# Splitting a weight load by rows, meant for the DMA engines that end first, a shorter last load, and one output store in place of two

## The chip, the cores and the metric

The kernel runs on one core of one Trainium2 chip. The metric is the device time of one execution in microseconds (us), the median of several runs. A profiled execution also has a *span*, from the first to the last instruction that the profile counts; the span is about 2.1 us shorter than the device time. A run is called fast when it lies within 1.5% of the fastest of the same kernel.

## The reference, cut to what matters

```python
# A: 32 heads, 32768 keys each; B: 32 query heads, 8 key/value heads, the last 4096 keys
q = (x @ wq) ...                        # one token
p = softmax(q @ k_cache^T * Dh ** -0.5)
o = p @ v_cache
return o.reshape(1, 1, 4096) @ wo       # wo: 4096 x 512, once for A and once for B
# out = concat([a, b], axis=-1)         # 1 x 1 x 1024, bf16
```

Nearly all of the time goes into reading the caches of A, 537 MB. The change touches only what comes after: the 4 MB of `A_wo` and the 512 outputs of A.

## The kernel before

All large loads are issued by SyncE (SP) into one DMA queue, one behind the other (q1 of the page: 570.43 of 570.59 MB). `A_wo` lies in SBUF as 128 partitions ("rows") of 32 chunks, 512 bf16 values (1 KB) per chunk and row. It is loaded in five parts, cut along the chunks, so that TensorE (PE) can start on a part when that part has landed.

```python
    def load(self, dst, src, sem, *deps):
        self.op("sp", lambda e: e.dma_start(dst, src).then_inc(sem, 16), *deps)

    WO_CUTS = {"A": (0, 11, 19, 25, 29, 32), "B": (0, 16, 32)}

    def load_wo(self, name, part):
        a0, a1 = self.WO_CUTS[name][part:part + 2]
        src = self.X[name]["wo"].rearrange("(p a) c -> p (a c)", a=32)
        ...
        self.load(self.kbuf[:, off + 512 * a0:off + 512 * a1], src[:, 512 * a0:512 * a1], self.wosem[name][part],
                  self.free["k"][t])
```

The projection works off the parts in turn. Part 0 of A goes as full-width matmuls into a bank of its own (line 745 of the kernel before, 746 after). The later chunks go as two half-width matmuls side by side, into partitions 0 and 64 of one bank (`halves`, line 719 before, 724 after). Ahead of part 3 the result of part 0 is added in by an fp32 matmul. Each half is then cast into SBUF, one by VectorE (DVE) and one by ScalarE (ACT), and stored by a DMA of its own.

```python
    def store(self, bank, i, dep):
        row = slice(64 * i, 64 * i + 1)
        out, src = self.out_sb[row, :], bank[row, 0:256]
        if i == 0:
            o = self.op("dve", lambda v: v.tensor_copy(out, src), dep)
        else:
            o = self.op("act", lambda e: e.activation(out=out, in_=src, func=ACTF.Copy), dep)
        self.op("act" if i else "sp", lambda e: e.dma_start(self.out[0, :, 256 * i:256 * i + 256], out).then_inc(
            self.outsem[f"A{i}"], 16), o)

    def emit_proj(self):
        ...
        for part in range(1, len(self.WO_CUTS["A"]) - 1):
            if part == 3:
                ...                                          # adds part 0's row, fp32
            self.proj_part("A", part, ...)                   # waits for wosem["A"][part] >= 16
        for i in range(2):
            o = self.op("pe", ...halves(..., oz[:, 31:32], wo[:, 512 * 31:512 * 32], False, True, (i,)), ...)
            self.store(self.PT, i, o)
```

## Time and profile before

| What | Before | From |
|---|---|---|
| device time, median of the first 3 runs | 1323.75 us (1323.66 to 1323.96) | timed runs |
| span | 1321.6 us | profile page |
| read from HBM | 570.43 MB, 432 GB/s over the span | profile page |
| PE / DVE busy | 73% / 57% | profile page |
| landings of the last `A_wo` part, 16 DMA engines | 1317.05 to 1318.85 us | the trace's semaphore records |
| last landing to the start of the DVE cast | 0.57 us | the same, and the timeline |
| start of the cast to the end of the span | 2.17 us | timeline |

A *landing* is a mark on a load's semaphore in the trace. A load of 128 rows has 16 of them here, as many as there are DMA engines; I read each as the arrival of one engine's share. A *packet* is one DMA transfer as the trace records it; in the loads of `A_wo` and `B_wo` it is one row's piece (part 1 of `A_wo`: 128 packets of 8 KB, each 309 ns). From the first landing of part 0 to the first of part 1 it is 2.45 us (1310.56 to 1313.01), and from last to last the same (1312.37 to 1314.82): about eight packets of 309 ns, so eight rows to a landing is my estimate. Which engine moves which rows, and which engine leaves which mark, the trace does not tell.

The lines of the profile page that tell what bounds the kernel, the span in 40 equal slices; `DMA` is the busy share of the 16 DMA engines in tenths (9 is 90% or more), `GB/s` what they moved:

```profile
span 1321.6 us, 28783 instructions
...
DMA  9999999999999999999999999999999999999998
GB/s 402 435 436 429 440 432 430 440 434 432 435 434 434 432 436 438 428 436 436 428 438 434 428 438 434 428 440 432 431 440 432 434 434 432 436 432 434 440 428 365
```

The kernel is bound by its loads from end to end.

The tail in stretches of 4 us; the columns are length, then busy time (instructions) of PE, its weight loads, DVE, ACT and GpSimd, then the granted TensorE clock (the share of its full clock that TensorE was allowed), the DMA engines' busy share and GB/s:

```profile
core 0: us, PE busy (x) PEld busy (x) DVE busy (x) ACT busy (x) POOL busy (x), PEclk, DMA share, GB/s
1306.00:1310.00 4.00, 1.66 (x28) 0.70 (x20) 1.90 (x6) 0.00 (x0) 0.00 (x0) 1.00 1.01 429
1310.00:1314.00 4.00, 3.13 (x39) 1.08 (x40) 0.88 (x2) 0.00 (x0) 0.00 (x0) 1.00 0.99 420
1314.00:1318.00 4.00, 4.00 (x41) 2.04 (x41) 1.36 (x2) 0.00 (x0) 0.00 (x0) 1.00 0.89 367
```

The chain that ended last, its end, in order of time (start, length, what):

```profile
1313.97 2.27 PE psT L745 x11
1316.24 3.15 PE psPT L719 x42
1319.39 0.02 issue
1319.42 0.41 DVE out_sb L727
```

And the timeline of the tail (start, length, engine, line, operation; SPq and ACTq are DMA issues):

```profile
1318.33 1.06 PE L719 MATMUL psPT<-kbuf,oz_A 128*1 128x256 bf16 x14
1319.42 0.41 DVE L727 CAST out_sb<-psPT 1x256 bf16<-1x256 f32 x1 [2.36 <-PE psPT L719]
1319.45 0.38 ACT L729 ACTIVATE out_sb<-psPT 1x256 bf16<-1x256 f32 x1 [18.04 <-PE psPT L719]
1319.86 0.25 SPq L730 DMA_DIRECT2D out_dram<-out_sb  x1
1319.86 0.58 ACTq L730 DMA_DIRECT2D out_dram<-out_sb  x1
```

The chain names PE and no DMA, but the landing at 1318.85 lies inside its `3.15 PE` piece: the last six matmuls start at 1318.89. PE and the loads end together. The two stores are issued together, and ACT's issue takes 0.33 us longer than SP's.

### The profile page before, as it was taken

How to read it: one execution, taken by the hardware profiler on the slowest of the kernel's cores; microseconds unless marked ns; L12 is line 12 of the kernel's file. 1: busy time of each engine (PE TensorE's matmuls, PEld its weight loads, DVE VectorE, ACT ScalarE, POOL GpSimd, SP SyncE). 2: the span in 40 equal slices, each digit the busy share in tenths (PEclk: the TensorE clock that was granted, in tenths of full speed). 3: DMA queues.
4: the chain of work that ended last, by engine and by line, in shares of the span. 5: the costliest groups of instructions: out<-in, count | busy, mean ns of one | idle time of the engine just before them, and what ended most of it. 6: DMA issues, size and time to landing. Idle time of an engine off the chain costs nothing. (4 is left out here: it accounts for less than half of the span.)

```text
span 1321.6 us, 28783 instructions
## 1 busy us (share of the span) xinstructions
PE 969.7 (73%) x13243; PEld 676.6 (51%) x13243; DVE 751.8 (57%) x1341; ACT 55.2 (4%) x168; POOL 2.6 (0%) x22
## 2 busy tenths in 40 slices
PE   4675768777677878776787777678777667877787
PEld 3353446555444655544465544445554445555453
DVE  3563556664555666455566645556665456665564
ACT  0000000000000000000000000000000000000000
POOL 0000000000000000000000000000000000000000
PEclk9886788887878888788888878888887788888788
DMA  9999999999999999999999999999999999999998
GB/s 402 435 436 429 440 432 430 440 434 432 435 434 434 432 436 438 428 436 436 428 438 434 428 438 434 428 440 432 431 440 432 434 434 432 436 432 434 440 428 365
DMA packets 13217, 570.59 MB, mean 432 GB/s; under 512 B 1555, under 2 KB 1558, under 8 KB 1942
## 3 DMA queue, kind: packets, MB, share of 16 engines
q1 hardware_dynamic: 12916, 570.43, 99.8%
q8 instruction: 8, 0.13, 0.0%
q10 hardware_dynamic: 290, 0.00, 0.0%
q14 instruction: 3, 0.02, 0.0%
HBM read 570.43 MB, written 0.00 MB: 432 GB/s over the span
## 5 line engine op out<-in xcount | busy, mean ns | idle before, releaser
L557 DVE COPY kt<-psT 128x1024 bf16<-128x1024 bf16 x1056 | 655.3, 684 | 235.9 <-PE psT L553 234.3
L553 PE MATMUL psT<-ident,kbuf 128*128 128x128 bf16 x8448 | 580.3, 234 | 166.6 <-DMA kbuf<-in_A_k_cache_dram 152.5
L553 PEld LDWEIGHTS psT<-ident,kbuf 128*128 128x128 bf16 x8448 | 540.7, 106 | 258.8 <-DMA kbuf<-in_A_k_cache_dram 160.5
L656 PE MATMUL psACC<-vbuf,ptsb 128*4 128x512 bf16 (+1 forms) x2112 | 187.4, 532 | 22.8 <-ACT ptsb L631 22.0
L576 PE MATMUL psS<-kt,qw 128*32 128x512 bf16 x2048 | 157.7, 385 | 14.8 <-DVE kt L557 14.8
L670 DVE TENSOR_SCALAR oc_A<-psACC,hot_A 128x128 f32<-128x128 f32 x32 | 11.2, 351 | 252.1 <-PE psG L683 252.1
L656 PEld LDWEIGHTS psACC<-vbuf,ptsb 128*4 128x4 bf16 (+1 forms) x2112 | 60.5, 111 | 140.1 <-issue 93.1
L604 ACT ACTIVATE psb<-psS,nb_A 128x512 bf16<-128x512 f32 x32 | 22.0, 687 | 1167.4 <-DVE nb_A L603 1167.4
L576 PEld LDWEIGHTS psS<-kt,qw 128*32 128x32 bf16 x2048 | 34.1, 95 | 57.3 <-DVE kt L557 30.4
L683 PE MATMUL psG<-oc_A,hw 128*32 128x128 f32 (+1 forms) x128 | 19.3, 227 | 52.3 <-DVE oc_A L672 52.3
L683 PEld LDWEIGHTS psG<-oc_A,hw 128*32 128x32 f32 x128 | 11.4, 109 | 62.4 <-DVE oc_A L672 55.0
L628 PE MATMUL psPT<-ident,psb 128*128 128x128 bf16 x136 | 18.2, 278 | 34.0 <-ACT psb L604 34.0
L672 DVE SCALAR_TENSOR_TENSOR oc_A<-psACC,hot_A,oc_A 128x128 f32<-128x128 f32 x96 | 33.7, 351 | 3.4
L593 DVE TENSOR_REDUCE tr_in<-psS 128x1 f32<-128x512 f32 x34 | 23.5, 692 | 17.2 <-PE psS L576 17.2
L628 PEld LDWEIGHTS psPT<-ident,psb 128*128 128x128 bf16 x136 | 10.3, 119 | 37.1 <-ACT psb L604 36.7
L597 PE MATMUL psACC<-rows,tr_in 128*1 128x64 f32 x64 | 8.7, 218 | 25.6 <-DVE tr_in L593 25.6
L631 ACT ACTIVATE ptsb<-psPT 128x512 bf16<-128x512 bf16 x34 | 20.3, 597 | 30.7 <-PE psPT L628 30.7
L597 PEld LDWEIGHTS psACC<-rows,tr_in 128*1 128x1 f32 x64 | 2.7, 81 | 35.1 <-DVE tr_in L593 35.1
L601 PE MATMUL psACC<-mr_A,nscale 1*128 1x1 f32 x64 | 12.1, 256 | 9.8 <-DVE mr_A L600 9.8
L601 PEld LDWEIGHTS psACC<-mr_A,nscale 1*128 1x128 f32 x64 | 9.4, 182 | 15.7 <-DVE mr_A L600 15.7
L495 PE MATMUL psACC<-vbuf,x_B 128*2 128x512 bf16 x32 | 3.6, 625 | 13.7 <-DMA x_B<-in_B_x_dram 13.7
L603 DVE COPY nb_A<-psACC 128x1 f32<-128x1 f32 x32 | 5.0, 158 | 15.0 <-PE psACC L601 15.0
(82 smaller groups left out, 76.5 us busy)
## 6 DMA issues: line engine op xcount, KB each, us to landing
kbuf<-in_A_k_cache_dram SPq DMA_DIRECT2D x4, 4096.0 KB, 23.1
kbuf<-in_B_k_cache_dram SPq DMA_DIRECT2D x2, 4096.0 KB, 31.9
vbuf<-in_B_v_cache_dram SPq DMA_DIRECT2D x2, 4096.0 KB, 25.2
vbuf<-in_B_wq_dram SPq DMA_DIRECT2D x1, 4096.0 KB, 12.7
vbuf<-in_A_wq_dram SPq DMA_DIRECT2D x1, 4096.0 KB, 32.3
kbuf<-in_B_wo_dram SPq DMA_DIRECT2D x2, 2048.0 KB, 33.0
kbuf<-in_A_wo_dram SPq DMA_DIRECT2D x1, 1408.0 KB, 26.1
kbuf<-in_A_wo_dram SPq DMA_DIRECT2D x1, 1024.0 KB, 28.2
```

The source lines that it names most:

```text
L553: inst = e.transpose(T[:, 128 * k:128 * k + 128], src[:, DH * k:DH * k + DH], self.ident[:, :])
L557: self.copies.append(self.op("dve", lambda v: v.tensor_copy(KT[:, :], T[:, :]), o, to="pe"))
L576: inst = e.matmul(self.S[32 * c:32 * c + 32, :], lhsT=win, rhs=self.kt[(bb + c // 2) % NKT][:, 512 * (c % 2):512 * (c % 2) + 512], start=b ...
L593: o = dve(lambda v: v.reduce_max(tr["in"][:, 0:1], self.S[:, :], axis=AXX), self.sdone, self.k_pool, to="pe" if name == "A" else None)
L597: o = self.op("pe", lambda e: e.matmul(self.ACC[0:1, 0:64], lhsT=tr["in"][:, 0:1], rhs=self.rows64[:, :], start=True, stop=True, skip_grou ...
L601: o = self.op("pe", lambda e: e.matmul(self.ACC[:, 64:65], lhsT=self.nscale[:, :], rhs=t["mr"][0:1, :], start=True, stop=True, skip_group_ ...
L604: self.sread = self.op("act", lambda s: s.activation(out=self.psb[:, :], in_=self.S[:, :], func=ACTF.Exp, bias=t["nb"][:, k:k + 1], scale= ...
L628: inst = e.transpose(PT[:, 128 * jj:128 * jj + 128], self.psb[:, 128 * jj:128 * jj + 128], self.ident[:, :])
L631: self.ptread = self.op("act", lambda s: s.activation(out=self.ptsb[:, :], in_=PT[:, 0:512], func=ACTF.Copy), self.psread, to="pe")
L656: inst = e.matmul(acc[32 * c:32 * c + rows, 0:512], lhsT=lhsT, rhs=rhs, start=begin, stop=end, tile_position=(0, 32 * c), skip_group_check ...
L672: o = self.op("dve", lambda v, src=src, hot=hot: v.scalar_tensor_tensor(out=oc, in0=src, scalar=hot, in1=oc, op0=ALU.mult, op1=ALU.add), p ...
L683: return self.op("pe", lambda e: e.matmul(self.G[0:32, c0 + c:c0 + c2], lhsT=win, rhs=t["oc"][g % len(t["oc"])][:, c:c2], start=False, sto ...
```

## The change

Its intent: the 16 DMA engines do not end together (1.8 us apart), so give the ones that end first more of the last weights, and the ones that end last fewer. Rows 112 to 127 of part 0 go as DMAs of 5, 5 and 6 rows, which are meant to run only on engines that end first. The new cuts leave one chunk for the last load, so that less work follows the last landing. One 1 KB store by SP replaces two of 512 bytes, one of which was issued slowly by ACT (0.58 us, against SP's 0.25).

```diff
-        self.out_sb = sb("out_sb", [128, 256], BF16)
+        self.out_sb = sb("out_sb", [1, 512], BF16)
...
-    WO_CUTS = {"A": (0, 11, 19, 25, 29, 32), "B": (0, 16, 32)}
+    WO_CUTS = {"A": (0, 8, 17, 25, 29, 31, 32), "B": (0, 16, 32)}
...
-        self.load(self.kbuf[:, off + 512 * a0:off + 512 * a1], src[:, 512 * a0:512 * a1], self.wosem[name][part],
-                  self.free["k"][t])
+        for r0, r1 in zip(rows := self.wo_rows(name, part), rows[1:]):
+            self.load(self.kbuf[r0:r1, off + 512 * a0:off + 512 * a1], src[r0:r1, 512 * a0:512 * a1],
+                      self.wosem[name][part], self.free["k"][t])
+
+    def wo_rows(self, name, part):
+
+        return (0, 112, 117, 122, 128) if (name, part) == ("A", 0) else (0, 128)
...
-        deps = (self.wosem[name][part], 16), self.c[name]["ozop"]
+        deps = (self.wosem[name][part], 16 * len(self.wo_rows(name, part)) - 16), self.c[name]["ozop"]
...
-        self.op("act" if i else "sp", lambda e: e.dma_start(self.out[0, :, 256 * i:256 * i + 256], out).then_inc(
-            self.outsem[f"A{i}"], 16), o)
...
+        self.op("sp", lambda e: e.dma_start(self.out[0, :, 0:512], self.out_sb[:, :]).then_inc(self.outsem["A"], 16), *done)
```

More of the change, by code (lines that the diff above doesn't have):

```diff
@@ L318, in alloc @@
         self.wosem = {n: [s(f"wosem_{n}{i}") for i in range(len(self.WO_CUTS[n]) - 1)] for n in self.X}
-        self.outsem = {n: s(f"outsem_{n}") for n in ("B", "A0", "A1")}
+        self.outsem = {n: s(f"outsem_{n}") for n in self.X}
     def load(self, dst, src, sem, *deps):
@@ L723, in store @@
     def store(self, bank, i, dep):
-        row = slice(64 * i, 64 * i + 1)
-        out, src = self.out_sb[row, :], bank[row, 0:256]
+        out, src = self.out_sb[0:1, 256 * i:256 * i + 256], bank[64 * i:64 * i + 1, 0:256]
         if i == 0:
-            o = self.op("dve", lambda v: v.tensor_copy(out, src), dep)
-        else:
-            o = self.op("act", lambda e: e.activation(out=out, in_=src, func=ACTF.Copy), dep)
-        self.op("act" if i else "sp", lambda e: e.dma_start(self.out[0, :, 256 * i:256 * i + 256], out).then_inc(
-            self.outsem[f"A{i}"], 16), o)
+            return self.op("dve", lambda v: v.tensor_copy(out, src), dep)
+        return self.op("act", lambda e: e.activation(out=out, in_=src, func=ACTF.Copy), dep)
     def emit_proj(self):
@@ L753, in emit_proj @@
         oz, wo = self.c["A"]["oz"], self.kbuf[:, HALF * DH * self.wo_third("A"):]
+        done = []
         for i in range(2):
@@ L756, in emit_proj @@
                         (self.wosem["A"][-1], 16), self.c["A"]["ozop"])
-            self.store(self.PT, i, o)
+            done.append(self.store(self.PT, i, o))
+        self.op("sp", lambda e: e.dma_start(self.out[0, :, 0:512], self.out_sb[:, :]).then_inc(self.outsem["A"], 16), *done)
 _INS = ['A_x', 'A_k_cache', 'A_v_cache', 'A_wq', 'A_wo', 'B_x', 'B_k_cache', 'B_v_cache', 'B_wq', 'B_wo']
```

## The prediction

> **What bounds it now.** The page's slices show the DMA engines 90% or more busy in 39 of 40 slices, 432 GB/s over the span of 1321.6 us, 570 MB read. PE is 73% busy, DVE 57%. The loop streams loads and is left alone; only the last output weights (A_wo) and the tail move. What is in play lies after 1309 us.
>
> **The tail, from the trace's records.** The 16 DMA engines don't finish together. The landing marks of the last A_wo part come from 1317.05 to 1318.85 us: seven by 1317.78, one at 1318.11, eight from 1318.50. Every load since 41 us has this spread (1.8 us). The B store's one 1 KB packet starts at 1317.01, just as the earliest engine finishes. [...]
> After the last landing at 1318.85, PE does three chunks (two half-width matmuls side by side, 0.109 us a chunk; the last starts at 1319.11), the casts start at 1319.42 (DVE) and 1319.45 (ACT), both stores issue at 1319.86. SP's takes 0.25 us to issue and lands at 1320.93, ACT's takes 0.58 us and lands at 1321.11. The span ends 0.47 us later.
>
> **Costs.**
> 1. Rows: [...] An 8 KB row takes 0.306 us (landings of part 0 to part 1: 2.45 us for 8). With the new cuts (8, 9, 8, 4, 2, 1 chunks; small rows cost a few ns more each) the late engines finish 0.27 us earlier, at about 1318.58; the early ones 0.65 us later, 1317.7 to 1318.3, still before them.
> 2. Last load of one chunk: two chunks' matmuls (0.22 us) leave the end. But PE then has little slack. Worked forward from 1313.81 us: 8 wide chunks at 0.216, 17 chunks at 0.109, the fp32 row add 0.62, then 4+2 chunks; it reaches the last chunk at about 1318.66, 0.05 to 0.1 us after the landing. So the last matmul starts about 0.45 us earlier than before (1319.11), not 0.49.
> 3. One store from SP: saves ACT's slow issue, 0.18 us at the landing; waiting for both casts costs up to 0.03.
> 4. Four more DMA issues on SP, 0.4 us each, 20 us before they matter: free.
>
> Sum: 0.45 + 0.17, about 0.6 us of the tail, all on the critical path: 1323.1 us, 0.05% faster.
>
> **What would show it.** Last landing at 1318.5 to 1318.65 with a spread of about 1 us or less; last PE chunk at about 1318.66; one 1 KB store packet about 0.7 us after its issue.
>
> **What would make it wrong.** Rows grouped by seven, or rows 112 to 127 through low engines, may run slower than eights do (no trace here shows it). [...] Moved code may shift the instruction-fetch packets (16 KB, 0.9 us each) that probably made the spread. Run-to-run noise is 0.3 us, half the gain.
>
> Predicted 1323.15 us, range 1322.7 to 1323.7; over 2% faster 0.005, within 2% 0.99, over 2% slower 0.005.

How the rows fall to numbered engines, no trace here shows: I took it that the engines that end last would move seven rows of part 0 in place of eight, and those that end first up to ten ("low engines", here and in the expectations, are the latter). The 0.27 us of cost 1, which is part of the 0.45, was my estimate: one 8 KB row less (0.306 us), less a few ns for each smaller row (in the trace of before a 1 KB packet takes 46 ns, where an eighth of the 309 ns of 8 KB would be 39). That the instruction-fetch packets made the spread was a guess: the spread is 0.82 us in the load that lands from 22 us and 1.94 us in the one from 32 us, and the first of the eight 16 KB packets (0.92 us) starts at 30.5 us.

## The result, and the profile after

The changed kernel takes 1326.77 us (median of 6 runs, 1326.60 to 1327.56), the kernel before, of the same rounds and the first three, 1323.96 us (6 runs, 1323.66 to 1324.73). The ratio is 1.0021 with a 95% interval of 1.0008 to 1.0034: slower by 2.8 us, where 0.6 us of gain was forecast. A ratio here is the mean time of one kernel's fast runs over that of the other's fast runs of the same rounds, so it is not quite the ratio of the medians quoted.

The loop is unchanged (434 GB/s from 100 to 1270 us, before and after), and the page shows no loss until its last slice:

```profile
span 1324.9 us, 28793 instructions
...
DMA  9999999999999999999999999999999999999998
GB/s 405 432 443 430 431 441 429 435 433 437 432 431 441 429 439 429 435 433 431 441 429 439 431 433 437 427 441 429 439 431 433 437 427 439 433 437 431 430 440 317
```

The last slice moved at 317 GB/s in place of 365, while the busy row still reads 8. The stretches of the tail, with the columns of before:

```profile
1306.00:1310.00 4.00, 1.58 (x28) 0.70 (x23) 2.09 (x7) 0.00 (x0) 0.00 (x0) 1.00 1.03 274
1310.00:1314.00 4.00, 2.30 (x26) 0.37 (x18) 0.92 (x2) 0.00 (x0) 0.00 (x0) 1.00 0.99 208
1314.00:1318.00 4.00, 2.34 (x6) 0.73 (x7) 0.45 (x1) 0.00 (x0) 0.00 (x0) 0.64 0.97 369
1318.00:1322.00 4.00, 3.48 (x43) 1.72 (x43) 0.68 (x1) 0.00 (x0) 0.00 (x0) 0.93 0.86 346
```

From 1310 to 1314 us the engines are as busy as before (share 0.99) and move 208 GB/s where they moved 420. They are not idle: their packets take longer. In the trace's packet records of before, from 1305 us on, every 8 KB packet takes 309 ns and every 16 KB packet 611 ns. In the changed kernel 120 of the 256 packets of 8 KB take more than 400 ns, up to 864, and the 16 KB packets of `B_wo`, whose DMA is not changed at all, take up to 1328 ns where they overlap with the split one. The stretch begins just after part 0 begins to flow: its first 8 KB packet starts at 1306.70 us, and 8 KB packets longer than 309 ns start from 1307.27 us on. The semaphore of part 0 shows 35 marks, three of them early, at 1285.84, 1286.19 and 1286.53 us, 0.1 to 0.2 us after the issues of the small DMAs end. The 35 fit 16 for the 112 rows and, for 5, 5 and 6 rows, as many as rows plus one each; that division is my reading, and no record names the engines.

The chain that ended last now goes through the DMA, and the timeline of the tail follows:

```profile
1286.80 33.61 DMA kbuf<-in_A_wo_dram
1320.41 0.04 issue
1320.45 2.44 PE psPT L724 x33
1322.90 0.02 issue
1322.92 0.41 DVE out_sb L731
```

```profile
1321.42 0.59 PE L724 MATMUL psPT<-pb,e 1*1 1x256 f32 x4
1321.94 0.75 PEld L724 LDWEIGHTS psPT<-kbuf,oz_A 128*1 128x1 bf16 x14 [0.44 <-DMA kbuf<-in_A_wo_dram]
1321.95 0.94 PE L724 MATMUL psPT<-kbuf,oz_A 128*1 128x256 bf16 x14
1322.92 0.41 DVE L731 CAST out_sb<-psPT 1x256 bf16<-1x256 f32 x1 [3.26 <-PE psPT L724]
1322.96 0.38 ACT L732 ACTIVATE out_sb<-psPT 1x256 bf16<-1x256 f32 x1 [22.56 <-PE psPT L724]
1323.42 0.26 SPq L760 DMA_DIRECT2D out_dram<-out_sb  x1
```

The difference of the spans, 3.3 us, is then complete:

| Term | Before | After | Difference |
|---|---|---|---|
| last landing of `A_wo` | 1318.85 us | 1322.57 us | +3.72 us |
| last landing to the start of the DVE cast | 0.57 us | 0.35 us | −0.22 us |
| start of the cast to the end of the span | 2.17 us | 2.00 us | −0.17 us |

So the short last load and the single store did what they were meant to do, and the loads became 3.7 us slower. Why is the question for the experiments.

### The profile page after: what moved, and what is told of

The parts are those of the page before. It is cut to its first block, busy times and chain, and to the rows that moved or that the text cites. A ratio compares the mean times of both kernels' runs of the same rounds, so it can differ in the third digit from the quotient of the medians.

```text
span 1324.9 us, 28793 instructions
## 1 busy us (share of the span) xinstructions
PE 970.0 (73%) x13246; PEld 677.0 (51%) x13246; DVE 752.0 (57%) x1341; ACT 55.2 (4%) x168; POOL 2.6 (0%) x22
```

## The experiments

Rival theories: **G**, the DMA of 112 rows (seven to an engine, if 16 share them evenly) slows the writes or reads; **S**, the three small DMAs do; **C**, the finer cuts do, together with SP's last issue, which took 7.2 us in the changed kernel (its nine `A_wo` issues took 10.42 us in all). Then, about the mechanism: **H**, the reads in HBM lie unfavourably; **W**, the side that writes SBUF is the cause. Within W: **A**, only groups of rows that are no multiple of four collide; **P**, the rate goes with the rows that one DMA writes: half of them at half the rate, and only the DMA of all 128 at the full one.

A and P are guesses: no run here shows how SBUF is written, or which engine writes which row.

The experiments came in three jobs, each with its own runs of the kernel before (medians 1323.65, 1323.83 and 1323.70 us).

### e1: whole rows again

```diff
-        return (0, 112, 117, 122, 128) if (name, part) == ("A", 0) else (0, 128)
+        return (0, 128)
```

> The changed kernel with part 0 of A_wo as one DMA of 128 rows again; the new cuts and the single store stay. If the row split makes the loss [...], all of it goes: every 8 KB packet takes 309 ns again, the part's last landing is back at about 1318.8 us, and the time is 0.3 to 0.7 us below the kernel before. If the finer cuts make it (theory C: 9 KB and 1 KB rows, and the last issue that held SP for 7.2 us), it stays about 3 us above.

Measured: 1323.44 us (5 runs, 1323.21 to 1324.19) against 1323.65 before; ratio 0.9999, interval 0.9985 to 1.0013. Every 8 KB packet takes 309 ns again. In its stretches:

```profile
1306.00:1310.00 4.00, 1.59 (x32) 0.80 (x24) 2.09 (x7) 0.00 (x0) 0.00 (x0) 1.00 0.97 413
1310.00:1314.00 4.00, 3.20 (x38) 0.98 (x31) 1.24 (x3) 0.00 (x0) 0.00 (x0) 1.00 1.00 425
```

425 GB/s in place of 208: the whole loss is the row split, and C falls. (The long last issue is no cause either: no `A_wo` issue of e2 or e3 below takes more than 0.44 us, and both have the loss.) From the last landing (1319.16 us) to the cast (1319.52) is 0.36 us, as after the change. The medians are 0.2 us apart, and the interval contains 1, so a gain is not shown.

### e2: the row split alone

The row split of the change, put into the kernel before with its old cuts and two stores.

> The kernel before with nothing but the row split on its first A_wo part (11 chunks, 11 KB rows). G and S: 3 to 5 us slower than before (rows are 11/8 as long as in the changed kernel, so the loss may be 11/8 as large). C: the same as before within 0.5 us.

Measured: 1329.58 us (4 runs, 1329.10 to 1330.84), 5.9 us above before; ratio 1.0043, interval 1.0028 to 1.0059.

```profile
1306.00:1310.00 4.00, 2.36 (x35) 0.95 (x28) 1.40 (x4) 0.00 (x0) 0.00 (x0) 0.87 1.03 299
1310.00:1314.00 4.00, 2.44 (x38) 0.91 (x38) 1.38 (x4) 0.00 (x0) 0.00 (x0) 1.00 0.99 220
1314.00:1318.00 4.00, 1.02 (x2) 0.09 (x2) 0.68 (x1) 0.00 (x0) 0.00 (x0) 0.91 0.96 253
1318.00:1322.00 4.00, 3.86 (x12) 1.16 (x13) 0.00 (x0) 0.00 (x0) 0.00 (x0) 0.50 0.96 396
```

The split is enough by itself. It costs more than the 3 to 5 us expected. The last landing is 5.4 us later (1324.23 us); on top of that, PE had waited for part 0 until 1318.1 us and then ran its matmuls at a granted clock of 0.50 (fourth line), so it ended behind the loads: the cast starts 2.3 us after the last landing (1326.56 us), where it was 0.57 us.

### e3: 112 rows and 16 rows

```diff
-        return (0, 112, 117, 122, 128) if (name, part) == ("A", 0) else (0, 128)
+        return (0, 112, 128) if (name, part) == ("A", 0) else (0, 128)
```

> The changed kernel with rows 0 to 111 as one DMA [...] and rows 112 to 127 as another [...]. G: still 2.5 to 3.5 us slower than before, packets of 8 KB at 500 ns and more. S: back to 0.3 to 0.7 us faster than before.

Measured: 1326.74 us (4 runs, 1326.65 to 1327.10), the time of the changed kernel; ratio 1.0023, interval 1.0007 to 1.0038.

```profile
1310.00:1314.00 4.00, 2.54 (x17) 0.49 (x18) 0.69 (x1) 0.00 (x0) 0.00 (x0) 0.60 1.00 230
```

Here the three small DMAs are gone, one DMA of 16 rows stands in their place, and the loss is all there. S falls: the three small DMAs neither cost nor gain anything that can be seen.

### e4: other reads, same writes

All 128 rows in one DMA, the source rows 28 KB apart in place of 32. Its output is wrong, which doesn't matter for the time.

```diff
+        if (name, part) == ("A", 0):
+            return bass.AP(src.tensor, 0, [[14336, 128], [1, 4096]])
```

> All 128 rows in one DMA, eight to an engine, but the source rows lie 28 KB apart and not 32[...]. Wrong result on purpose. If the distance of the reads in HBM makes the loss (theory H): 8 KB packets at 500 ns and more, about 3 us slower. If it is the side that writes (theory W[...]): like the run without the row split, packets at 309 ns, within 0.7 us of before.

Measured: 1323.43 us (one look), every 8 KB packet at 309 ns.

```profile
1310.00:1314.00 4.00, 3.20 (x26) 0.85 (x14) 1.37 (x2) 0.00 (x0) 0.00 (x0) 1.00 1.00 425
```

The idea was that reads 28 KB apart would put the engines' reads as far apart as in the split, if each engine takes neighbouring rows. The trace doesn't tell which rows an engine takes, so what is shown is only that such reads cost nothing. e5 doesn't need the assumption.

### e5: same writes, other reads

The changed kernel, its 112-row DMA reading 112 consecutive pieces of 8 KB. Its output is wrong, which doesn't matter for the time.

```diff
+        if (name, part) == ("A", 0) and r0 == 0:
+            return bass.AP(src.tensor, 0, [[4096, 112], [1, 4096]])
```

> The changed kernel, its 112-row DMA reading 112 rows of 8 KB that lie one after the other in HBM (the writes as in the changed kernel). Wrong result on purpose. Theory W (the side that writes): still slow, 8 KB packets at 500 ns and more, within 0.7 us of the changed kernel. Theory H (the pattern of the reads): the stretch goes or changes much, the time falls by 1 us or more.

Measured: 1326.66 us (one look), 8 KB packets up to 855 ns.

```profile
1310.00:1314.00 4.00, 2.64 (x18) 0.43 (x18) 0.69 (x1) 0.00 (x0) 0.00 (x0) 0.62 1.00 212
```

Quite another pattern of reads, the same loss: H falls as far as reading patterns go. That it is the writes (W) is what is left, not something seen.

### e6: 64 rows and 64 rows

```diff
+        return (0, 64, 128) if (name, part) == ("A", 0) else (0, 128)
```

> Part 0 as rows 0 to 63 and rows 64 to 127[...]. If any full 16-engine split with whole groups of four rows is free (theory A: only groups that aren't a multiple of four collide): packets at 309 ns, the time of the run without the row split. If each half of the partitions can be written at only half the rate [...]: 8 KB packets near 618 ns and about 2.5 us slower than without the split.

Measured: 1326.85 us (one look), 8 KB packets up to 708 ns.

```profile
1306.00:1310.00 4.00, 1.59 (x28) 0.59 (x22) 2.09 (x7) 0.00 (x0) 0.00 (x0) 1.00 1.01 322
1310.00:1314.00 4.00, 2.13 (x22) 0.37 (x18) 1.27 (x2) 0.00 (x0) 0.00 (x0) 1.00 1.06 232
```

Two DMAs of 64 rows (four to an engine, if 16 share them evenly) are slow as well, so A, as far as the rows are shared so, falls. 232 GB/s over a stretch that also holds pieces of the neighbouring parts (214 in its first half, 249 in its second) is near half of the 425 GB/s of e1. The sizes were not met exactly: P expected packets near 618 ns and 2.5 us of loss; the median of part 0's packets is 542 ns, and the run is 3.4 us above e1 (of another job).

### e7: 120 rows and 8 rows

```diff
+        return (0, 120, 128) if (name, part) == ("A", 0) else (0, 128)
```

> Part 0 as rows 0 to 119 [...] and rows 120 to 127 [...]. Theory A (groups that are no multiple of four collide): 8 KB packets at 309 ns and the time of the run without the split[...]. Theory P [...]: packets stretched to 500 ns and more, 2 to 3.5 us slower.

Measured: 1327.17 us (one look), 8 KB packets up to 1021 ns.

```profile
1310.00:1314.00 4.00, 3.20 (x34) 0.78 (x22) 0.69 (x1) 0.00 (x0) 0.00 (x0) 0.71 1.05 228
```

The split at 120 rows runs at about half rate too (228 GB/s, against 425 in e1). All splits of these rows that I tried (112, 120, 64) do, and the DMA of 128 rows does not.

### e12: twice the dose

```diff
+        return (0, 112, 128) if name == "A" and part < 2 else (0, 128)
```

> Twice the dose: parts 0 and 1 of A_wo (8 and 9 chunks) both as 112 and 16 rows. Theory P: the half-rate stretch lasts about twice as long; the loss against the run without the row split grows from 3.3 us to 6 to 8 us. A one-off cost of the odd DMA (set-up, queue) would leave it at 3 to 4 us.

Measured: 1330.64 us (one look, against 1323.47 for e11 of the same job): 7.2 us of loss, where one split part cost 3.3 (e3 less e1). The last landing came at 1325.37 us, with one split part (e3) at 1322.66 and with none (e11) at 1319.05: 3.6 us for the first dose and 2.7 for the second. The rest of the 7.2 us comes after the loads: the cast starts 1.15 us after the last landing (1326.51 us), because PE was granted a clock of 0.50 from 1322 to 1324 us and ran behind them.

```profile
1310.00:1314.00 4.00, 1.87 (x16) 0.37 (x16) 0.28 (x1) 0.00 (x0) 0.00 (x0) 0.66 0.95 200
1314.00:1318.00 4.00, 3.53 (x7) 0.70 (x8) 1.10 (x2) 0.00 (x0) 0.00 (x0) 0.50 0.99 213
```

The half-rate stretch now goes on to 1318 us. A price paid once would have left the loss at 3 to 4 us. A price for each odd DMA would also have doubled here; against it speaks e2, where the same four DMAs carry 11 chunks in place of 8 and the last landing comes 5.4 us later in place of 3.7. The loss grows with the bytes loaded this way, though not in strict proportion.

### e8 and e9: the aim of the change in another way

Seven chunks of part 0 over 128 rows, and the eighth as 125 rows, meant for five engines, and 3 rows. This keeps most of part 0 in the fast form and was meant to give five engines about 17 KB more and the others 8 KB less: my estimate, from 125 rows of 1 KB shared by five (25 KB each), where the 128-row form has about eight rows (8 KB) to a landing. No record shows that they did.

```diff
+        if (name, part) == ("A", 0):
+            return (0, 128, 0, 7), (0, 125, 7, 8), (125, 128, 7, 8)     # rows, chunks
+        return (0, 128, a0, a1),
```

> The aim of the change without the odd groups: seven chunks of part 0 over 128 rows, and the eighth as rows 0 to 124 [...] and rows 125 to 127 [...]. [...] If an engine's own rate is the limit (theory E): the last landing comes 0.2 to 0.3 us before that of the run without the split, and the spread of the last landings falls from 2.1 to about 1.2 us. If [...] (P): no engine's last landing comes more than 0.1 us earlier, and packets are stretched while the column is under way.

> The low-engine column once more, because its first profile had all engines some 13% slow between 1312 and 1318 us, where nothing odd was under way, so its landings could not be read. Theory E (the engine is the limit): last landing 0.2 to 0.3 us before the run without the row split of the same job, time about 0.2 us below it. Theory P [...]: last landing and time equal or later, by 0 to 0.4 us.

Measured: e8 1324.48 us (4 runs, 1323.49 to 1325.38; ratio 1.0002, interval 0.9985 to 1.0019), e9, the same kernel, 1324.78 us (5 runs, 1323.42 to 1325.68; ratio 1.0007, interval 0.9993 to 1.0020). In both profiles the data rate stays low after the column is through; e9:

```profile
1306.00:1310.00 4.00, 1.59 (x32) 0.77 (x27) 2.09 (x7) 0.00 (x0) 0.00 (x0) 1.00 1.00 409
1310.00:1314.00 4.00, 3.20 (x32) 0.98 (x25) 1.37 (x2) 0.00 (x0) 0.00 (x0) 1.00 1.00 346
1314.00:1318.00 4.00, 1.87 (x22) 0.78 (x20) 0.68 (x1) 0.00 (x0) 0.00 (x0) 1.00 0.99 350
```

The bytes seem to have moved to the early engines. At the last `B_wo` landing of e9, eight engines come early (up to 1308.29 us) and eight late (from 1308.45); at the last `A_wo` landing only three are early (up to 1318.72) and thirteen late (from 1319.10). This fits the guess that the 125 rows went to five of the early engines; the records do not name the engines. But the late ones did not gain: the last landing is at 1320.34 us, against 1319.05 in e11 of the same job. Both theories missed: E expected it earlier, P up to 0.4 us later, and it is 1.3 us later, because in this kernel every 8 KB packet of part 2, which is an ordinary 128-row DMA, takes 360 to 369 ns and not 309 (346 to 355 in e8); the 9 KB packets of part 1 have a median of 416 ns, against 347 in e11. The second profile rules out a single disturbed run; it does not tell the cause, and neither theory explains it. So P, even if right, does not explain all that an odd DMA does. Two things can be said: this way does not gain either, and several DMAs on one semaphore do not by themselves halve the rate, for the 7 KB packets of the 128-row DMA here have a median of 272 ns, about 7/8 of 309.

### e10 and e11: what is left of the change without the split

e10 is the kernel before with the single store alone; e11 is e1 once more.

```diff
 e10:
-    WO_CUTS = {"A": (0, 8, 17, 25, 29, 31, 32), "B": (0, 16, 32)}
+    WO_CUTS = {"A": (0, 11, 19, 25, 29, 32), "B": (0, 16, 32)}
```

> The kernel before with nothing but the single store. From the start of the DVE cast to the end of the span 1.98 us in place of 2.17 (as the run without the row split showed); the time 0.1 to 0.25 us below before, which may not stand out of the scatter. The wait from the last landing to the cast stays at about 0.57 us.

> New cuts and single store, whole rows, once more: the version that may beat both kernels. 0.2 to 0.5 us below before, 3 us below the changed kernel; last landing to cast 0.36 us.

Measured: before 1323.70 us (9 runs, 1323.55 to 1324.19), e10 1323.42 us (5 runs, 1323.25 to 1324.20; ratio 1.0000, interval 0.9986 to 1.0013), e11 1323.47 us (5 runs, 1323.31 to 1323.96; ratio 0.9998, interval 0.9984 to 1.0011). The tail of e10:

```profile
1318.64 0.49 PE L724 MATMUL psPT<-kbuf,oz_A 128*1 128x256 bf16 x6 [0.25 <-DMA kbuf<-in_A_wo_dram]
1319.16 0.41 DVE L731 CAST out_sb<-psPT 1x256 bf16<-1x256 f32 x1 [3.76 <-PE psPT L724]
1319.66 0.25 SPq L760 DMA_DIRECT2D out_dram<-out_sb  x1
```

From the last landing (1318.60 us) to the cast is 0.56 us, as before; from the cast to the end of the span (1321.2) about 2.0 us, as after. So the store gives its 0.17 us of the tail. The medians of e10 and e11 are 0.28 and 0.23 us below before, which fits, but single runs of one kernel differ by up to 1 us (0.95 in e10), and both intervals contain 1. No version here is shown to beat the kernel before. In the profile of e11 the last landing is 0.45 us later than in e10 (1319.05 against 1318.60), but 0.41 us of that stands already at the last `B_wo` landing (1309.20 against 1308.79), before any of the new cuts matters.

One expectation of e11 was missed: from its last landing to the cast (1319.88 us) it is 0.83 us and not 0.36, more than the 0.57 of before. Its stretch from 1310 us, and the matmuls of B from its timeline:

```profile
1310.00:1314.00 4.00, 3.20 (x33) 0.92 (x26) 0.72 (x2) 0.00 (x0) 0.00 (x0) 0.67 1.01 427
1309.73 3.33 PE L738 MATMUL psS<-kbuf,oz_B 128*1 128x512 bf16 x32
```

The loads ran at full rate, but the granted clock was 0.67 in this stretch (0.50 from 1310 to 1312 us), where e1 had 1.00, and the same 32 matmuls of B took 3.33 us in place of 1.90. PE then ended behind the loads. In this profile the short last load saved nothing.

## Why the prediction was wrong

Predicted 1323.15 us, range 1322.7 to 1323.7; measured 1326.77 us. Point by point:

- *What bounds the kernel; nothing changes before the tail.* Right. The page's data rates agree up to the last slice.
- *Cost 1, "the late engines finish 0.27 us earlier", from "an 8 KB row takes 0.306 us".* This is the step that failed, in sign as well as in size: the last landing came 3.72 us later. I took the 0.306 us as a property of a row and an engine, whatever row goes through whatever engine. It was measured on DMAs of 128 rows only. In the changed kernel, 8 KB packets took up to 0.864 us and the core's data rate fell to 208 GB/s, about half. Undoing the split alone brings the loads back (e1), the split alone makes the loss (e2), the two reading patterns tried don't matter (e4, e5), and neither do the small DMAs (e3).
- *Why.* Shown: the row split makes the loss, and it reaches beyond the split DMA. The rate halves at a busy share of 0.99 (208 GB/s for 420); the packets of the unchanged `B_wo` stretch as well while they overlap (up to 1328 ns for 611); and every one of the splits 112, 120 and 64 does it (200 to 232 GB/s). That the cause lies on the writing side is what is left when the two reading patterns are ruled out. P expected half the rate before e6 ran, and 232 GB/s was measured against 425; by what mechanism is not shown. The trace doesn't tell which engine writes which partition, so for 112 rows the size of the loss is measured and not derived.
- *Balance.* The prediction had the spread of the last landings fall to about 1 us. It stayed at 1.9 us (1320.70 to 1322.57).
- *Cost 2, the short last load.* Right in the saving after the last landing: 0.57 us became 0.35 us. That PE would reach the last chunk 0.05 to 0.1 us late could not be seen in the changed kernel, whose loads were late; in e1 the last chunk's matmuls start 0.05 us after the landing. In e11, the same kernel as e1, PE was granted less clock and the saving was gone (0.83 us): "PE then has little slack" was right, but the forecast reckoned with one clock, the 1.00 of the tail before.
- *Cost 3, the single store.* Right: 0.17 us from cast to end, 0.17 forecast, and the same alone in e10.
- *Cost 4, four more issues.* Right in effect. Eight of the nine issues took 0.26 to 0.43 us, but the last took 7.2 us, which was not foreseen, so that all nine took 10.42 us. They were over at 1295.4 us, 11 us before part 0 began to flow.
- *"What would make it wrong".* "Rows grouped by seven, or rows 112 to 127 through low engines, may run slower than eights do" named the cause, but as a remark: the range of 1322.7 to 1323.7 us gave it no room. A change of which rows go together, whose cost no trace at hand showed, asked for a wider range.

## What to carry to other kernels

A per-row or per-engine time measured on a full 128-row load need not hold for another split of the rows: here other splits halved the data rate of the whole core (200 to 232 GB/s for 420 to 427, 1310 to 1314 us), at a busy share of 0.95 to 1.06 where it was 0.99 to 1.01. Where a load must be cut, try columns first, as the parts of `A_wo` are cut; the cuts along the rows at 112, 120 and 64 each lost about 3 us here. When a change moves work between engines of a stream that is already at its limit, read GB/s and the times of the packets beside the busy share: here 8 KB packets went from 309 ns to as much as 864.
